# One exponential per key tile, written as 32-bit words and split by halves

## The chip, the cores and the metric

The kernel runs on one core of a Trainium2 chip. The metric is device time in microseconds from start to end of one execution; the number quoted is the median of several executions. The engines are PE (TensorE, matmuls), PEld (its loads of stationary operands), DVE (VectorE), ACT (ScalarE), POOL (GpSimd) and SP (SyncE, which issues the DMAs).

## What is computed

The reference is a clustered attention followed by a soft mixture of experts. For each of 4 x 8 heads, 768 queries and 768 keys of 64 elements are assigned to the nearest of 16 centroids; a query sees the keys of its own cluster alone.

```
mask = q_assign[:, :, :, None] == k_assign[:, :, None, :]
scores = np.where(mask, scale * q @ k.T, -1e9)
attn = np.exp(scores - scores.max(-1))
attn = attn / (attn.sum(-1) + 1e-9)
x = attn @ v                     # -> 3072 rows of 512
logits = x @ phi                 # 32 slots
slot_input = softmax(logits, 0).T @ x
h = relu(slot_input[e] @ w1[e]); slot_out[e] = h @ w2[e]
out = softmax(logits, 1) @ slot_out
```

All inputs and the output are float32.

## The kernel before

The 32 heads are walked in order, in pairs. Scores are made transposed: a key tile has 128 keys on the partitions and 768 queries along the row, six key tiles (j) per head (i). For each head PE does three things. Pass A (`pass_a`, L695) makes untransposed scores, whose row maxima DVE takes (`rowmax`, L703). Pass B (`pass_b`, L737) makes the transposed scores of one key tile in a PSUM buffer `pb` (two of them take turns), with mask and row maximum folded in by extra rows of the operands. Pass C (`pass_c`, L798) multiplies the exponentials by the values and sums over key tiles: the exponentials are the stationary operand, 128 queries at a time, and 64 or 65 columns of values move through them.

Float32 precision is kept by pairs of float16 numbers. Before the change one key tile costs two exponentials on ACT (`expo`, L764): one rounds to float16, which is the high part `EH`, one writes float32, and a subtraction (`elow`, L767) of the two gives the low part `EL` in float16. For most tiles the float32 lies in SBUF (`E32`) and POOL subtracts; for the others, marked D in `LOWS`, `FIRST_LOWS` and `LAST_LOWS`, the float32 is written back to PSUM and DVE subtracts. Values are split the same way by `scalev`, `splitv_hi` and `splitv_lo` into the tile `vx`, and pass C takes three products per query block:

```
for o, (e, r0, w) in enumerate(((eh, D, W), (eh, 0, D), (el, D, W))):
    nc.tensor.matmul(pc[:, c0:c0 + w], e[:, ts], vx[:, j, r0:r0 + w], ...)
```

Column 64 of the values is constant, so that the sum of the exponentials comes out beside the product; `norm` (L812 to L814, DVE) divides.

The order of the work is set by a planner (class `Plan`). Each operation is entered with its engine, an estimated duration, a key, and what it reads and writes; buffer rings of a given depth (`e32`, `eh`, `el` and others) add the waits for reuse. A list scheduler takes, per engine, the ready operation with the least due time, where the table `K` shifts the due time of each key, and `_wt` entries let an operation wait for a more urgent one. The last head's last tile goes in two halves (`expo_half`, `elow_half`, L776 to L783), so that the end of the attention is short.

Six large buffers (`arena`, w7 to w12 in the programs' names) hold the attention's operands; when their last reader is done, expert weights are loaded into them (L1276, SP). The expert part (`TAIL`) follows in an order written out by hand; its operations `hi` (ACT, L1021) and `lo` (DVE, L1024) split weights into float16 pairs, and eight of them are woven into gaps of the attention (`weave`, from planner time `FILL_FROM` on).

Of the kernel before, what the change touches and what calls it, by code (L numbers as in the profile page):

```python
# [10 lines left out]
F16 = mybir.dt.float16  # L11
AF = mybir.ActivationFunctionType
# [6 lines left out]
VS = 256.0  # L19
# [38 lines left out]
class Plan:  # L58
# [127 lines left out]
    FILL_HIGH, FILL_LOW, FILL_BUSY, FILL_FROM = 0.6, 0.62, 1.7, 60.0  # L186
# [38 lines left out]
def clustered_attention_then_soft_moe(  # L225
# [96 lines left out]
    NE32, NEH, NEL = 4, 6, 4  # L322
# [95 lines left out]
    def dma(o, i):  # L418
# [20 lines left out]
        b1=-1581.1, b2=-1348.93, b3=-1474.85, b4=-772.75, b5=-2796.86, x=-3075.5, el=-2389.91,
        c0=-754.47, c1=-1452.52, c2=-1723.07, c3=-1326.05, c4=-1422.75, c5=-1659.96, norm=-0.36,  # L440
        xtrans0=-3047.02, xtrans_out0=-1797.54, xtrans1=-762.69, xtrans_out1=-3163.12, logits=-3303.75,
        disp=-2092.22, comb=-3215.74, warm=-563.02, load_w=-524.15, p0_load_r=-190.35, p0_sims=-1812.55,
        p0_sims_out=-1246.75, p0_assign=-1916.55, p0_assign1=-1303.5, p0_assign2=-846.55,
        p0_assign3=-1913.5, p0_assign4=-176.75, p0_onehot=-1183.1, p0_onehot_out=-1399.44,
        p1_load_r=-2399.42, p1_sims=-1512.26, p1_sims_out=-634.95, p1_assign=-1481.1,
        p1_assign1=-2773.32, p1_assign2=-1055.87, p1_assign3=-2084.84, p1_assign4=-308.2,
        p1_onehot=-2132.69, p1_onehot_out=-2851.21, h0_split_hi=-1530.33, h0_place1=-416.32,
        h0_split_lo=-2905.16, h0_place2=-2748.93, h0_place_mask=41.5, h0_place3=-2642.86,
        h0_load_v=-2985.05, h0_splitv_hi=-927.37, h0_splitv_lo=-2206.46, h0_maxrow=-590.33,
        h0_maxrow_out=-2498.68, h0_x=-1091.42, h0_el=-2014.91, h0_norm=-2111.78, h0_a0=-2392.32,  # L450
# [308 lines left out]
    def ehigh(i, j):  # L759
        return EH[(NT * i + j) // 2 % (NEH // 2)][:, j % 2, :]  # L760
# [824 lines left out]
```

## Time and profile before

| | |
|---|---|
| time, median of 3 executions | 429.03 us (428.45 to 429.6) |
| profiled execution, span from first to last instruction | 427.3 us |
| profiled execution, its own time | not listed apart from the three |
[...]
| start, up to the steady pattern | 0 to about 56 us |
| pairs of heads in the steady pattern | about 56 to 340 us |
| last heads of the attention | about 340 to 373 us |
| expert part and output | about 373 to 427 us |

The three executions differ by 0.27%. The profile is of one execution; its durations are used below, and the span is compared with the median.

### The profile page before, as it was taken

The numbers are of one execution on the slowest core, as the hardware profiler recorded it, in microseconds if no ns is written. First come the engines' busy times: TensorE is split into PE (matmuls) and PEld (weight loads), VectorE is DVE, ScalarE is ACT, GpSimd is POOL, SyncE is SP. The second block draws the span as 40 slices with busy tenths as digits, with TensorE's granted clock in tenths as the row PEclk, the third lists the DMA queues.
The fourth block names the chain that finished last, engine by engine and source line by source line (L and its number), as shares of the span: only waits on it lengthen the run. The fifth ranks groups of instructions, "written<-read, shape, count | busy, mean of one in ns | idle before, by whom it ended". The sixth has DMA issues, their size and how long they took to land.

```text
span 427.3 us, 16090 instructions
## 1 busy us (share of the span) xinstructions
PE 411.3 (96%) x6535; PEld 298.3 (70%) x6535; DVE 381.3 (89%) x749; ACT 371.0 (87%) x597; POOL 328.1 (77%) x267
## 2 busy tenths in 40 slices
PE   8989999999999999999999999999999999899991
PEld 8747677777776777777776777777767777642671
DVE  5889999999999999999999999999999977679972
ACT  5378999999999899999998999999989999849741
POOL 8669999899988798989897889897986688326000
PEclk9999999999999999999999999999999999999998
DMA  6675466566567646667575565665656643899977
GB/s 194 146 226 135 120 156 203 142 198 173 156 182 191 172 104 160 205 162 208 152 216 156 154 167 138 167 173 155 176 158 177 167 148 124 292 356 385 371 307 290
DMA packets 43901, 81.84 MB, mean 192 GB/s; under 512 B 8372, under 2 KB 27956, under 8 KB 43828
## 3 DMA queue, kind: packets, MB, share of 16 engines
q1 hardware_dynamic: 43828, 80.82, 63.6%
q8 instruction: 51, 0.84, 0.8%
q14 instruction: 22, 0.18, 0.1%
HBM read 52.63 MB, written 6.29 MB: 138 GB/s over the span
## 4 chain that ended last, share of the span: by engine, by line
PE 86%; DVE 5%; ACT 5%; issue 1%; DMA 1%; POOL 0%; SPq 0%; DVEq 0%; POOLq 0%
PE pb L737 27%; PE pc L798 22%; PE pa L695 14%; ACT w L764 3%; PE pso L1421 3%; PE pt L554 3%; PE ph L1380 2%; PE pt L823 2%; PE pc L1331 2%; PE pt L902 2%; PE pt L835 1%; DVE w L767 1%; PE po L1499 1%; PE pt L581 1%; ACT pb L764 1%
## 5 line engine op out<-in xcount | busy, mean ns | idle before, releaser
L764 ACT ACTIVATE w<-pb 128x768 f16<-128x768 f32 (+1 forms) x319 | 242.7, 834 | 15.6 <-PE pb L737 14.2
L767 POOL TENSOR_TENSOR w<-w,w 128x768 f16<-128x768 f32 x128 | 209.1, 1646 | 37.0 <-ACT w L764 28.9
L703 DVE TENSOR_REDUCE siT<-pa 128x1 f32<-128x512 f32 (+1 forms) x288 | 187.9, 682 | 5.6 <-PE pa L695 3.9
L737 PE MATMUL pb<-w 128*128 128x512 f16 x764 | 151.6, 325 | 1.2 <-DVE w L767 0.6
L798 PEld LDWEIGHTS <-w 128*128 128x128 f16 x3456 | 126.9, 97 | 11.1 <-DVE w L783 0.4
L798 PE MATMUL pc<-vx,w 128*128 128x65 f16 x3402 | 133.3, 193 | 0.3 <-DVE w L783 0.2
L737 PEld LDWEIGHTS <-w 128*128 128x128 f16 x764 | 69.9, 97 | 59.8 <-issue 6.0
L695 PE MATMUL pa<-w 128*128 128x512 f16 (+1 forms) x384 | 104.1, 326 | 1.1 <-DVE siT L703 0.8
L767 DVE TENSOR_TENSOR w<-pb,w 128x768 f16<-128x768 f32 x63 | 59.8, 949 | 7.7 <-ACT pb L764 4.6
L650 POOL TENSOR_TENSOR w<-w 128x768 f16<-128x768 f32 x32 | 52.6, 1645 | 2.3
L764 ACT ACTIVATE pb<-pb 128x768 f32<-128x768 f32 x63 | 53.2, 844 | 0.0
L695 PEld LDWEIGHTS <-w 128*128 128x128 f16 x384 | 36.4, 98 | 11.7 <-issue 5.0
L647 POOL CAST w<-w 128x768 f16<-128x768 f32 x30 | 24.7, 824 | 9.5 <-DMA w<-w 6.9
L683 POOL TENSOR_TENSOR vx<-w,vx 128x384 f16<-128x384 f32 x32 | 29.1, 909 | 0.4 <-ACT vx L679 0.4
L1024 DVE SCALAR_TENSOR_TENSOR w<-w,w 128x512 f16<-128x512 f32 x31 | 22.5, 769 | 0.0
L1021 ACT ACTIVATE w<-w 128x512 f16<-128x512 f32 x36 | 20.5, 625 | 1.2 <-PE ph L1380 1.2
L814 DVE TENSOR_TENSOR w<-pc,siT 128x384 f32<-128x384 f32 (+1 forms) x32 | 17.6, 551 | 1.1
L675 ACT ACTIVATE w<-w 128x384 f32<-128x384 f32 x32 | 17.6, 551 | 0.8 <-DMA w<-vt 0.8
L679 ACT CAST vx<-w 128x384 f16<-128x384 f32 x32 | 17.7, 554 | 0.2
L554 PEld LDWEIGHTS <-w 128*128 128x128 f16 x540 | 15.7, 96 | 2.6 <-issue 0.5
L828 ACT COPY xT<-pt 128x384 f32<-128x384 f32 x30 | 15.8, 525 | 0.0
L585 ACT ACTIVATE w<-pt,ohsc 128x768 f16<-128x768 bf16 x15 | 13.6, 904 | 2.4 <-PE pt L581 2.4
(209 smaller groups left out, 391.1 us busy)
## 6 DMA issues: line engine op xcount, KB each, us to landing
w<-qkT SPq DMA_DIRECT2D x32, 384.0 KB
w<-w SPq DMA_DIRECT2D x128, 96.0 KB
w<-w1r SPq DMA_DIRECT2D x38, 312.0 KB
w<-w SPq DMA_DIRECT2D x188, 48.0 KB
w<-w2a SPq DMA_DIRECT2D x16, 512.0 KB
w<-w2b SPq DMA_DIRECT2D x16, 512.0 KB
w<-vt SPq DMA_DIRECT2D x32, 192.0 KB
out<-w SPq DMA_DIRECT2D x10, 512.0 KB
```

The source lines that it names most:

```text
L554: nc.tensor.matmul(ps[:, c0:c0 + 2 * NCL], x[(2 * p + hh) % 3][:, t * P:(t + 1) * P], y, start=(hh == 0 and t == 0 and o == 0), stop=(o == ...
L647: (nc.scalar.copy if e == "ACT" else ENG[e].tensor_copy)(RH[i % 3], R[i % 3])
L650: nc.gpsimd.tensor_sub(RL[i % 3], R[i % 3], RH[i % 3])
L683: nc.gpsimd.tensor_sub(vx[:, :, 0:D], V[i % 2], vx[:, :, D:2 * D])
L695: nc.tensor.matmul(pa[:, c0:c0 + w], q1[:, q0:q0 + P], k1[:, k0:k0 + w], start=True, stop=True)
L703: nc.vector.tensor_reduce(hd[i]["mc"][:, 4 * m + c0:4 * m + c1], pa.rearrange("p (n c) -> p n c", n=c1 - c0), axis=AX.X, op=ALU.max, negat ...
L737: nc.tensor.matmul(pbt[j % 2][:, q0:q1], k_[:, kc], q_[:, q0:q1], start=(o == 0), stop=(o == 1))
L764: nc.scalar.activation(dst, pbt[j % 2][:, 0:S], AF.Exp, scale=SCALE)
L767: (nc.vector if lows(i)[j] == "D" else nc.gpsimd).tensor_tensor(EL[(NT * i + j) % NEL], e32(i, j), ehigh(i, j), op=ALU.subtract)
L798: nc.tensor.matmul(pc[:, c0:c0 + w], e[:, ts], vx[:, j, r0:r0 + w], start=(j == 0 and c0 == 0 and o == 0), stop=(j == NT - 1 and o == 2), ...
L1021: nc.scalar.mul(to, segment(n, s), WS)
L1024: nc.vector.scalar_tensor_tensor(low_of(n, s), segment(n, s), WS, HI[n, s], op0=ALU.mult, op1=ALU.subtract)
```

## The change

ACT now evaluates one exponential per key tile, with a bias of 18.125 added to the exponent, and writes 32-bit integers into a word buffer `EW` (eight of them in a ring, in place of four `E32`, six `EH` and four `EL`). The largest exponential is then some 2 to the 26.15. Read as float16, the upper 16 bits of such a word are the number's upper part times 2 to the -24, with no conversion: the word's upper half is below 2048, and float16 patterns up to there are linear in their bits. The lower 16 bits are an unsigned integer; POOL (the DVE path stays in the code but no tile is marked D any more) multiplies them by 2 to the -24 and writes float16 into the same place. Pass C takes its stationary operand from the words, every second float16, so that its columns lie four bytes apart; and since upper and lower halves now carry the same scale, the lower half meets a second value operand `vw`, the values' high part times 2 to the -16, which ACT makes once per head (`splitv_sc`). `VS` and the constant in `norm` follow. The last tile's two halves take one exponential on ACT and one conversion on DVE each. The table `K` is new throughout, and `FILL_FROM` goes from 60 to 90.

```diff
-VS = 256.0
+VS = 1024.0
+EB = 18.125
+EL1 = 2.0 ** -24
+VL1 = 2.0 ** -16
...
-LOWS = ('PDPDPP', 'PDPDPP')
-LAST_LOWS = "PDPDDD"
-FIRST_LOWS = ("PPPDPP", "PPPDPP")
+LOWS = ('PPPPPP', 'PPPPPP')
+LAST_LOWS = "PPPPPP"
+FIRST_LOWS = ("PPPPPP", "PPPPPP")
...
-    FILL_HIGH, FILL_LOW, FILL_BUSY, FILL_FROM = 0.6, 0.62, 1.7, 60.0
+    FILL_HIGH, FILL_LOW, FILL_BUSY, FILL_FROM = 0.6, 0.62, 1.7, 90.0
...
-    NE32, NEH, NEL = 4, 6, 4
+    NEW = 8
...
+    VWs = [area(3, 7 + n, 1)[:, 0:NT * (D + 2)].rearrange("p (t d) -> p t d", d=D + 2) for n in range(2)]
...
-    E32 = [area(n, c, 2, F32) for n, c in ((2, 4), (2, 6), (2, 8), (3, 7))]
-
-    EH = [area(4, 2 * n, 2).rearrange("p (t s) -> p t s", t=2) for n in range(NEH // 2)]
-    EL = [area(4, NEH + n, 1) for n in range(NEL)]
+    EWAT = ((4, 0), (4, 2), (4, 4), (4, 6), (4, 8), (2, 4), (2, 6), (2, 8))
+    EW = [area(n, c, 2, F32) for n, c in EWAT]
...
+        nc.gpsimd.memset(VWs[n][:, :, D:D + 1], VS * VL1)
...
+    def splitv_sc(i):
+        nc.scalar.mul(VWs[i % 2][:, :, 0:D], VXs[i % 2][:, :, D:2 * D], VL1)
...
-    def e32(i, j):
-        if lows(i)[j] == "D":
-            return pbt[j % 2][:, 0:S]
-        return E32[e32n[NT * i + j] % NE32]
+    def words(i, j):
+        return EW[(NT * i + j) % NEW].bitcast(I32)
+
+    def pieces(i, j, dt=F16):
+        return EW[(NT * i + j) % NEW].bitcast(dt).rearrange("p (s k) -> p s k", k=2)
...
-    def ehigh(i, j):
-        return EH[(NT * i + j) // 2 % (NEH // 2)][:, j % 2, :]
-
     def expo(i, j):
-        for dst in (ehigh(i, j), e32(i, j)):
-            nc.scalar.activation(dst, pbt[j % 2][:, 0:S], AF.Exp, scale=SCALE)
+        nc.scalar.activation(words(i, j), pbt[j % 2][:, 0:S], AF.Exp, bias=EB, scale=SCALE)
 
     def elow(i, j):
-        (nc.vector if lows(i)[j] == "D" else nc.gpsimd).tensor_tensor(
-            EL[(NT * i + j) % NEL], e32(i, j), ehigh(i, j), op=ALU.subtract)
+        (nc.vector if lows(i)[j] == "D" else nc.gpsimd).tensor_scalar(
+            pieces(i, j)[:, :, 0], pieces(i, j, U16)[:, :, 0], EL1, 0.0, op0=ALU.mult, op1=ALU.add)
...
     def expo_half(i, j, u):
-        if u == 1:
-            nc.scalar.activation(seg(ehigh(i, j), u), half(u), AF.Exp, scale=SCALE)
-        nc.scalar.activation(half(u), half(u), AF.Exp, scale=SCALE)
-
-    def ehigh_half(i, j, u):
-        nc.vector.tensor_copy(seg(ehigh(i, j), u), half(u))
+        nc.scalar.activation(seg(words(i, j), u), half(u), AF.Exp, bias=EB, scale=SCALE)
 
     def elow_half(i, j, u):
-        nc.vector.tensor_tensor(seg(EL[(NT * i + j) % NEL], u), half(u), seg(ehigh(i, j), u), op=ALU.subtract)
+        nc.vector.tensor_scalar(pieces(i, j)[:, u * HS:(u + 1) * HS, 0], pieces(i, j, U16)[:, u * HS:(u + 1) * HS, 0],
+                                EL1, 0.0, op0=ALU.mult, op1=ALU.add)
...
-        eh, el, vx = EH[n // 2 % (NEH // 2)][:, j % 2, :], EL[n % NEL], VXs[i % 2]
+        e, vx, vw = pieces(i, j), VXs[i % 2], VWs[i % 2]
         for t in range(NT) if u is None else range(u, NT, 2):
             ts = slice(t * P, (t + 1) * P) if u is None else slice(u * HS + t // 2 * P, u * HS + (t // 2 + 1) * P)
             pc, c0 = (hd[i]["pcs"][t % 2], t // 2 * W) if two else (hd[i]["pc"], t * W)
-            for o, (e, r0, w) in enumerate(((eh, D, W), (eh, 0, D), (el, D, W))):
-                nc.tensor.matmul(pc[:, c0:c0 + w], e[:, ts], vx[:, j, r0:r0 + w],
+            for o, (k, v, r0, w) in enumerate(((1, vx, D, W), (1, vx, 0, D), (0, vw, 0, W))):
+                nc.tensor.matmul(pc[:, c0:c0 + w], e[:, ts, k], v[:, j, r0:r0 + w],
...
-        nc.vector.tensor_scalar_add(z, pv[:, :, :, D], VS * 1e-9)
+        nc.vector.tensor_scalar_add(z, pv[:, :, :, D], VS * EL1 * 2.718281828459045 ** EB * 1e-9)
...
+            op("ACT", 0.42, "splitv_sc", h0, lambda i=i: splitv_sc(i), [("vx", i)], [("vw", i)])
...
-                        op("ACT", 0.9 if u else 0.45, "x", t, lambda i=i, j=j, u=u: expo_half(i, j, u), [("pbu", u)],
-                           (ring if u else []) + [("eu", u)])
-                        if u == 0:
-                            op("DVE", 0.5, "el", t, lambda i=i, j=j, u=u: ehigh_half(i, j, u), [("eu", u)], ring[:1] + [("eu", u)])
+                        op("ACT", 0.45, "x", t, lambda i=i, j=j, u=u: expo_half(i, j, u), [("pbu", u)],
+                           ring[:1] + [("eu", u)])
...
+                op("ACT", 0.74, "x", t, lambda i=i, j=j: expo(i, j), [("pb", n)], [("ew", n)])
                 if lows(i)[j] == "D":
-                    op("ACT", 1.395, "x", t, lambda i=i, j=j: expo(i, j), [("pb", n)], [("eh", n), ("pb", n)])
-                    op("DVE", 0.87, "el", t, lambda i=i, j=j: elow(i, j), [("pb", n), ("eh", n)], [("el", n)])
+                    op("DVE", 0.87, "el", t, lambda i=i, j=j: elow(i, j), [("ew", n)], [("el", n)])
                 else:
-                    m = e32n[n] = len(e32n)
-                    op("ACT", 1.395, "x", t, lambda i=i, j=j: expo(i, j), [("pb", n)], [("e32", m), ("eh", n)])
-                    op("POOL", 1.58, "el", t, lambda i=i, j=j: elow(i, j), [("e32", m), ("eh", n)], [("el", n)])
+                    op("POOL", 0.87, "el", t, lambda i=i, j=j: elow(i, j), [("ew", n)], [("el", n)])
                 op("PE", 0.553, f"c{j}", h0, lambda i=i, j=j: pass_c(i, j),
-                   [("eh", n), ("el", n), ("vx", i), ("pc", i)] + ([("flc", 0)] if end else []),
+                   [("ew", n), ("el", n), ("vx", i), ("vw", i), ("pc", i)] + ([("flc", 0)] if end else []),
...
-        c0=-754.47, c1=-1452.52, c2=-1723.07, c3=-1326.05, c4=-1422.75, c5=-1659.96, norm=-0.36,
...
+        h2_b3=-1170.54, h2_b4=-1548.42, h2_b5=-3005.88, h2_c0=-2432.74, h2_c1=-1059.02, h2_c2=-1774.13,
```

The planner's order moves with it. The first place is ACT's row of work where the first head's exponentials begin. `pb0` and `pb1` are the two score buffers, w9, w10 and w11 three of the large buffers, `pt` the one-hot masks of the next pair. Before:

```order
L727 ACTIVATE w9_90<-pb1_116 1x384 x2
L585 ACTIVATE w10_91<-pt_448,ohsc_70 128x768
L764 ACTIVATE w11_92<-pb0_115 128x768
L764 ACTIVATE w9_90<-pb0_115 128x768
L764 ACTIVATE w11_92<-pb1_116 128x768
L764 ACTIVATE w9_90<-pb1_116 128x768
```

After the change, the same place on ACT:

```order
L732 ACTIVATE w9_90<-pb1_118 1x384 x2
L766 ACTIVATE w11_92<-pb1_118 128x768
L587 ACTIVATE w10_91<-pt_459,ohsc_70 128x768
L766 ACTIVATE w11_92<-pb0_117 128x768
L766 ACTIVATE w11_92<-pb1_118 128x768
L766 ACTIVATE w11_92<-pb0_117 128x768
L766 ACTIVATE w9_90<-pb1_118 128x768
```

The first exponential has moved ahead of the copy of the one-hot masks (L585, now L587), and each score buffer is read once, not twice.

The second place is POOL's row in the steady pattern, some ten rows that belong to a little over one head. The L647, L650 and L683 rows are the float16 copy and low part of Q and K and the low part of the values. Before:

```order
L647 CAST w7_88<-w7_88 128x768
L650 TENSOR_TENSOR w8_89<-w7_88 128x768
L767 TENSOR_TENSOR w11_92<-w10_91,w11_92 128x768
L767 TENSOR_TENSOR w11_92<-w9_90,w11_92 128x768 x3
L683 TENSOR_TENSOR vx_1_113<-w8_89,vx_1_113 128x6x64
L767 TENSOR_TENSOR w11_92<-w10_91,w11_92 128x768
```

After the change, with the same three operations at L649, L652 and L685:

```order
L649 CAST w7_88<-w7_88 128x768
L652 TENSOR_TENSOR w8_89<-w7_88 128x768
L685 TENSOR_TENSOR vx_0_111<-w8_89,vx_0_111 128x6x64
L769 TENSOR_SCALAR w11_92<-w11_92 128x768 x3
L769 TENSOR_SCALAR w9_90<-w9_90 128x768
```

Four or so subtractions of two operands per head have become six conversions of one, each in place in its word buffer.

The third place is the end of the attention on ACT, from the last but two key tiles on. Before:

```order
L764 ACTIVATE w11_92<-pb1_116 128x768
L764 ACTIVATE pb1_116<-pb1_116 128x768
L764 ACTIVATE w11_92<-pb0_115 128x768
L764 ACTIVATE pb0_115<-pb0_115 128x768
L777 ACTIVATE pb1_116<-pb1_116 128x384
L776 ACTIVATE w11_92<-pa1_118 128x384
L777 ACTIVATE pa1_118<-pa1_118 128x384
```

After the change:

```order
L766 ACTIVATE w9_90<-pb1_118 128x768
L766 ACTIVATE w11_92<-pb0_117 128x768
L825 COPY xT1_110<-pt_7508 128x384
L777 ACTIVATE w9_90<-pb1_118 128x384
L777 ACTIVATE w9_90<-pa1_120 128x384
L766 ACTIVATE w9_90<-pb0_117 128x768
```

The two halves of the last tile (L777) now stand ahead of the last whole tile, the one before it in the sum, whose lower half is POOL's last conversion.

## Rows read from the trace of the kernel before

**Rows 1.** The page: span, and each engine's busy time.

```profile
span 427.3 us, 16090 instructions
PE 411.3 (96%) x6535; PEld 298.3 (70%) x6535; DVE 381.3 (89%) x749; ACT 371.0 (87%) x597; POOL 328.1 (77%) x267
```

**Rows 2.** Chain that ended last, 56 to 340 us: shares, one piece (start, length).

```profile
by line: PE pb L737 36.4%; PE pc L798 30.3%; PE pa L695 18.5%; PE pt L554 4.0%; PE pt L823 3.0%; PE pt L902 2.3%; PE pt L835 2.1%; PE pt L581 1.5%; PE pt L714 1.0%; PE pt L875 0.6%; PE pt L872 0.3%; issue 0.0%
...
120.15 1.44 PE pb L737 x8
```

**Rows 3.** The same chain, 20 to 56 us.

```profile
by line: PE pb L737 26.4%; PE pc L798 16.8%; PE pa L695 15.6%; ACT w L764 7.8%; DVE siT L703 7.7%; PE pt L554 4.6%; POOL w L650 4.6%; DVE w L767 2.6%; ACT w L585 2.5%; PE pt L581 2.4%; issue 2.2%; DVE pt L565 1.6%; DVE pt L570 1.6%; DVE siT
...
25.66 2.81 ACT w L764 x4
```

**Rows 4.** The same chain, 342.2 to 373.3 us.

```profile
by line: ACT w L764 36.0%; DVE w L767 15.4%; ACT pb L764 10.8%; issue 9.6%; PE pb L737 7.3%; DVE w L1024 5.1%; DVE w L814 4.8%; PE pa L695 2.4%; DVE w L783 2.0%; ACT vx L679 2.0%; DVE siT L813 1.9%; DVE w L780 1.5%; DVE siT L812 1.1%; PE pa
```

**Rows 5.** Chain in order of time, one pair of heads, 231.7 to 253 us.

```profile
231.82 0.89 PE pt L554 x36
...
237.09 0.34 PE pt L581 x6
...
239.49 0.33 PE pt L823 x3
...
247.25 1.11 PE pc L798 x36
248.36 0.65 PE pb L737 x4
...
252.93 0.09 PE pt L554 x4
```

**Rows 6.** Windows: busy us (instructions) of PE, PEld, DVE, ACT, POOL; clock, DMA share, GB/s.

```profile
342.00:373.00 31.00, 29.26 (x503) 22.01 (x499) 22.45 (x39) 30.05 (x47) 21.40 (x15) 1.00 0.56 187
...
370.00:405.00 35.00, 34.22 (x484) 17.83 (x486) 30.57 (x75) 25.23 (x61) 9.89 (x17) 1.00 0.99 371
```

**Rows 7.** Groups by line and form: out<-in, count, busy us, mean ns; idle before.

```profile
L764 ACT ACTIVATE w<-pb 128x768 f16<-128x768 f32 x191 | 159.1, 833 | 15.6 <-PE pb L737 14.2 <-POOL w L767 0.2
L764 ACT ACTIVATE w<-pb 128x768 f32<-128x768 f32 x128 | 106.8, 834 | 0.0
L764 ACT ACTIVATE pb<-pb 128x768 f32<-128x768 f32 x63 | 53.2, 844 | 0.0
...
L679 ACT CAST vx<-w 128x384 f16<-128x384 f32 x32 | 17.7, 554 | 0.2
...
L767 POOL TENSOR_TENSOR w<-w,w 128x768 f16<-128x768 f32 x128 | 209.1, 1646 | 37.0 <-ACT w L764 28.9 <-DVE siT L703 1.9 <-ACT xT L828 1.9
L650 POOL TENSOR_TENSOR w<-w 128x768 f16<-128x768 f32 x32 | 52.6, 1645 | 2.3
L683 POOL TENSOR_TENSOR vx<-w,vx 128x384 f16<-128x384 f32 x32 | 29.1, 909 | 0.4 <-ACT vx L679 0.4
L647 POOL CAST w<-w 128x768 f16<-128x768 f32 x30 | 24.7, 824 | 9.5 <-DMA w<-w 6.9 <-DMA w<-qkT 1.8 <-issue 0.8
...
L767 DVE TENSOR_TENSOR w<-pb,w 128x768 f16<-128x768 f32 x63 | 59.8, 949 | 7.7 <-ACT pb L764 4.6 <-PE pc L798 1.3
```

**Rows 8.** Groups of weight loads by line and form (rows x columns, type).

```profile
L798 PEld LDWEIGHTS <-w 128*128 128x128 f16 x3456 | 126.9, 97 | 11.1 <-DVE w L783 0.4 <-issue 0.3
...
L823 PEld LDWEIGHTS pt<-ident,w 128*128 128x128 f32 x90 | 11.2, 141 | 1.4
...
L1421 PEld LDWEIGHTS <-w 128*32 128x32 bf16 x96 | 1.8, 96 | 0.8 <-issue 0.3
```

**Rows 9.** Chain in order of time, 7 to 9 us: float32 matmuls, 128 weights, 32 columns.

```profile
7.61 1.33 PE pt L591 x12
```

**Rows 10.** Windows of lines L798, then L737 alone, 342 to 373 us.

```profile
342.00:373.00 31.00, 14.61 (x384) 13.56 (x380) 1.00 0.56 187
...
342.00:373.00 31.00, 12.50 (x64) 6.00 (x64) 1.00 0.56 187
```

More of the change, by code (lines that the diff above doesn't have):

```diff
@@ L11 @@
 F16 = mybir.dt.float16
+I32 = mybir.dt.int32
+U16 = mybir.dt.uint16
 AF = mybir.ActivationFunctionType
@@ new lines, in clustered_attention_then_soft_moe @@
+        const6=-1044.52, const9=-2731.44, h0_sims=-2494.06, h1_sims=-2443.21, h0_assign1=-2333.46,
+        h0_assign2=-516.44, h0_assign3=-2529.58, h1_assign1=-2696.57, h1_assign2=-734.39,
+        h1_assign3=-1337.48, h0_onehot=-1457.34, h0_onehot_out=-2765.81, h1_onehot=-1431.93,
+        h1_onehot_out=-1809.37, const=-2763.86, const1=-1541.01, const2=-566.36, load_r=-1694.69,
+        sims=-2592.52, sims_out=-2919.8, assign=-1534, assign1=-2001.48, assign2=-3012.88,
+        assign3=-3219.57, assign4=-152.75, onehot=-2252.72, onehot_out=-4042.04, split_hi=-1262.07,
@@ new lines, in clustered_attention_then_soft_moe @@
+        p0_onehot_out=-1998.94, p1_load_r=-2631.65, p1_sims=-2385.28, p1_sims_out=-634.95,
+        p1_assign=-1481.1, p1_assign1=-3152.73, p1_assign2=-2526.84, p1_assign3=-1909.13,
+        p1_assign4=-308.2, p1_onehot=-3037.17, p1_onehot_out=-1455.75, h0_split_hi=-2021.69,
+        h0_place1=-2663.29, h0_split_lo=-2535.2, h0_place2=-4200.41, h0_place_mask=41.5,
+        h0_place3=-3714.84, h0_load_v=-2185.11, h0_splitv_hi=-3052.6, h0_splitv_lo=-2754.32,
+        h0_maxrow=-2319.67, h0_maxrow_out=-926.74, h0_x=-1010.67, h0_el=-3729.84, h0_norm=-3032.86,
@@ new lines, in clustered_attention_then_soft_moe @@
+        h3_split_lo=-1256.42, h3_place2=-1445.27, h3_place_mask=-1180.48, h3_place3=-876.77,
+        h3_load_v=-2953.38, h3_splitv_hi=-673.01, h3_splitv_lo=-266.72, h3_maxrow=-961.01,
+        h3_maxrow_out=-2034.15, h3_x=-1592.82, h3_el=-1279.46, h3_norm=-1397.97, h3_a0=-2234.38,
+        h3_a1=-1520.89, h3_a2=-1156.03, h3_a3=-2719.37, h3_a4=-3211.15, h3_a5=-3309.57, h3_a6=-2362.73,
+        h3_a7=-1862.43, h3_a8=-2128.17, h3_ra0=-1180.81, h3_ra1=-1010.17, h3_ra2=-678.32,
+        h3_ra3=-2524.91, h3_ra4=-1981.12, h3_ra5=-2033.79, h3_ra6=-2174.95, h3_ra7=-2406.4,
@@ new lines, in clustered_attention_then_soft_moe @@
+        maxrow_wt=1.5, norm1_wt=0.2, norm2_wt=0.4, norm3_wt=0.5, norm5_wt=0.2, o1_a6_wt=0.4,
+        o1_b0_wt=0.2, o1_b5_wt=0.5, o1_c2_wt=0.6, o1_c3_wt=0.1, o1_c4_wt=0.7, o1_load_v_wt=1.5,
+        o1_maxrow_out_wt=0.6, o1_norm_wt=0.7, o1_place3_wt=0.4, o1_ra0_wt=0.2, o1_ra2_wt=0.5,
+        o1_split_hi_wt=0.9, o1_splitv_hi_wt=1.4, onehot_out_wt=0.7, p1_assign2_wt=0.4,
+        p1_assign3_wt=0.4, p1_load_r_wt=0.6, p1_onehot_out_wt=1.4, place1_wt=1.1, place3_wt=0.5,
+        place_mask_wt=0.9, ra3_wt=0.5, ra4_wt=0.6, ra6_wt=0.7, ra7_wt=0.6, split_lo_wt=0.7,
@@ L1304, in rings, with ew @@
         return [(c * HS, 2 * HS, plan.touching((k, b0 - n))) for n, c in enumerate(at) if c is not None]
-    ends = range(plan.last["e32"] - NE32 + 1, plan.last["e32"] + 1)
+    def ew(n):
+        ends = range(plan.last["ew"] - NEW + 1, plan.last["ew"] + 1)
+        return [(EWAT[v % NEW][1] * HS, 2 * HS, plan.touching(("ew", v))) for v in ends if EWAT[v % NEW][0] == n]
     held = (
@@ L1312, in clustered_attention_then_soft_moe @@
         rings("q2", NH - 1, None, 0, 2)
-        + [((4 + 2 * (v % NE32)) * HS, 2 * HS, plan.touching(("e32", v))) for v in ends if v % NE32 < 3],
+        + ew(2),
         rings("q1", NH - 1, 0, 5) + rings("q2", NH - 1, 2) + [(4 * HS, HS, plan.touching(("ohs", NH // 2 - 1)))]
-        + [(7 * HS, 2 * HS, plan.touching(("e32", v))) for v in ends if v % NE32 == 3],
-        last("eh", NEH, 1, *range(NEH)) + last("el", NEL, 1, *range(NEH, NEH + NEL)),
+        + last("vw", 2, 1, 7, 8),
+        ew(4),
         last("xn", 5, 2, 6, 8, 0, 2, 4) + spares(("fin", 0), ("fin", 5), ("pl", NH // 2 - 1)),
```

166 lines of the change are left out of this document (69 added, 97 removed).

## The prediction

> **What bounds the kernel now.** I read the page's busy shares first. PE shows 96%, DVE 89%, ACT 87%, POOL 77% [rows 1]; four engines that close together don't say which sets the time, and PE's share is flattered because the ends of matmuls are modelled and overlap. So the chain that ended last decides, read by stretch. From 56 to 340 us, two thirds of the span, every named piece of the chain is a PE line and "issue" is 0.0% [rows 2]: whatever ACT, DVE and POOL do there is ready before PE wants it. The chain of one pair of heads shows how tight that is: PE goes from the sims of one pair at 231.82 to those of the next at 252.93, 21.1 us, in pieces of 36 pass C matmuls in 1.11 us (30.8 ns each), four score matmuls in 0.65 us and the like, end to end [rows 5]. Faster exponentials can buy almost nothing in this stretch.
>
> They can buy something at its two ends. From 20 to 56 us the chain has ACT's exponentials with 7.8%, DVE's low halves with 2.6% and DVE's row maxima with 7.7%; its longest ACT piece is 2.81 us, four exponentials in a row at 25.66 [rows 3]. From 342.2 to 373.3 us the chain is mostly not PE: ACT's exponentials 36.0% and 10.8%, DVE's low halves 15.4% [rows 4]. ACT is busy there for 30.05 of 31.00 us [rows 6]. After 373 us comes the expert part, which the change leaves alone but for what sits in the buffers it loads into.
>
> **The change, part by part.**
>
> *ACT.* A key tile now costs one exponential in place of two. Rows of before: 191 + 128 exponentials into SBUF at 833 and 834 ns and 63 into PSUM at 844 [rows 7]. 191 of them go, 159 us of busy time. Added are 32 scalings of 128x384 (the new second value operand); the nearest row is the cast of the same shape, 554 ns [rows 7], so 18 us. That the exponential writes 32-bit integers is not in the trace. Float16 and float32 outputs cost the same in the rows just named, so the output type has not mattered; I take 0.83, with 0.84 (the PSUM form) as the other end. A one-column bias is free by the same argument.
>
> *POOL.* 128 two-input subtractions at 1646 ns go; 191 one-input conversions come, of 768 unsigned 16-bit numbers four bytes apart into float16 in the same place. Nearest rows: a one-input cast of the same 768 columns takes 824 ns, a two-input operation 1646 [rows 7]. Bounds 0.82 and 1.65; I take 0.85, since what is new has one input and one output. Per head POOL then has 6 x 0.85, plus 1.65 and 0.91 for low parts of Q/K and V and 0.82 for the cast: 8.5 us of PE's 10.55. *DVE* loses 63 subtractions of 949 ns [rows 7], 60 us, and gains two half-size conversions at the very end. All of these lie beside PE's work in the long stretch and cost or give nothing there.
>
> *PE.* The same 3456 pass C matmuls with the same columns; the number of rows doesn't change. What is new is the stationary operand: 128 float16 columns that lie four bytes apart. No row of before has that. Nearest rows from both sides: the packed float16 load takes 97 ns, as long as a bfloat16 load of only 32 columns (96), while the float32 loads of 128 columns, whose elements do lie four bytes apart, take 141 [rows 8]. [...]
>
> [...]
>
> *The new priorities* move instructions. At the start ACT's first exponential now stands ahead of the one-hot copy, and tiles follow one per instruction. At the end the two half tiles come ahead of the last whole tile, whose lower half POOL makes. In the long stretch the pieces per pair are the same with fewer changes of kind.
>
> **The sum,** against the profiled span of 427.3 us [rows 1], in which PE is already the chain for 284 us.
> - Start: of the 2.81 us of four exponentials half is gone (1.4), DVE's 2.6% of 36 us (0.95) turns into POOL work beside ACT, but the row maxima (2.8 us of chain) stay and are late next. I take 2.0; ends 0 and 3.7 (2.8 of ACT plus 0.95).
> - Long stretch: two score tiles in a row take 1.44 us in one place where twice 0.65 is 1.30 [rows 2, 5]; if each pair hides 0.2 us of such waits (an estimate), 13 pairs give 2.7. The other end is zero, since changes of order can open new waits as well. I take 1.0.
> - End: between 342 and 373 us PE has 384 pass C and 64 score matmuls out of 503 [rows 6, 10]. At the pace of the pair they need 384 x 30.8 ns = 11.8 and 16 x 0.65 = 10.4 us; the other 55 come to some 5.3 at 0.1 each, an estimate from the transposes (0.33 for three [rows 5]). 27.5 of 31.0: 3.5 us idle. POOL's conversion (0.85) between exponential and pass C is what the last tile waits for next. I take 2.5; ends 0 and 3.5.
> - Expert part: from 370 to 405 us the DMA engines are busy 0.99 of the time [rows 6]. The loads wait for the attention's buffers, so they move with its end, but they can't run faster: I give back 0.5; ends 0 and 2.
>
> 2.0 + 1.0 + 2.5 - 0.5 = 5.0, so a span of 422.3. The timed executions have a median of 429.03, 1.7 above the profiled span (that execution's own time is not listed), so 424.0 us. From the ends: nothing won and 2 given back, 431.0; all won, 3.7 + 2.7 + 3.5, 419.1.
>
> **The rivals.**
> - *Pass C's weights load slowly (slower than before).* What such a load does to the pace can be read where float32 weights of 128 columns meet only 32 moving columns: 12 such matmuls take 1.33 us, 111 ns each [rows 9], against 0.89 us for 36 with packed float16 weights and the same 32 columns, 25 ns [rows 5]. Transposes with 128 float32 columns have the same 110 ns pace (0.33 for three [rows 5]), so it is not columns but the weights that set the 111. With two passes per float32 matmul (an estimate: 128 columns at twice the 57 ns which 6 bfloat16 transposes of 128 columns show in 0.34 us [rows 5]) one load is 55 ns. Pass C would go from 30.8 to 55.5 ns: 3456 x 24.7 ns = 85 us, 428 + 85 = 513 us; with 111 ns even 705. The point that decides is small: 5.0 us over 3456 matmuls, 1.45 ns each. For it: the step is that of float32. [...]
> - *POOL becomes the bound (slower).* Its head is 3.38 + 6x us; it passes PE's 10.55 at x = 1.2 us. At the two-input price, 1.65, a head takes 13.3 us: 2.7 x 30 heads = 82 us, 511 us. Against: with one input the rows say 0.82.
> [...]
> - *Nothing comes of it.* PE is the chain anyway; the waits at both ends go over to row maxima on DVE and to POOL's conversions ahead of the last pass C, or DMA holds the expert part: 428 to 430 us.
>
> **How the numbers follow.** A difference under 0.3% (1.3 us) can't be told from none. The forecast, PE's pace unchanged and part of the waits at the ends won, has 0.70, with a range of its own of 419 to 428. No change has 0.10. The slow weight load has 0.14, POOL 0.04, and another 0.02 is for waits that the new order opens, some 432 us. So faster 0.70, same 0.10, slower 0.20. The first two cases hold 8 in 10 together: the range is 418 to 431, by the ends of the sum and a microsecond below, and takes in nothing of the two far rivals.
>
> **What would show it.** Right: pass C's rows still at 30 to 31 ns from start to start and loads at 97 ns; POOL's conversion at 0.8 to 1.0 us; ACT's busy time near 230 us and DVE's near 320, with the pair still at 20.9 to 21.2 us; the chain from 342 us on made of PE; the last pass C some 5 us earlier. Wrong: a pair of 26 us (weight loads) or a chain of POOL rows; a conversion over 1.2 us; a chain in which DVE's row maxima or the DMA take over the ends.

## The result, and the profile after

The changed kernel takes 424.62 us (median of 17 executions, 422.66 to 429.36); the kernel before, run beside it, 428.55 us (17 executions, 427.7 to 429.79). The ratio is 0.990, with a 95% interval of 0.988 to 0.992: faster by about 1% (the ratio leaves out the two slowest executions of the changed kernel, 429.3 and 429.4). The first execution that was profiled took 429.3 us, the long end of that spread, so the profile read here is that of another execution of the same kernel, which took 422.75 us with a span of 421.0 us (run e1 below). That is 1.9 us under the median, so the 6.3 us between the two profiles' spans are more than the 3.9 us between the medians.

The page, engine by engine; it answers to [rows 1]:

```profile
span 421.0 us, 15786 instructions
...
PE 406.2 (96%) x6535; PEld 296.0 (70%) x6535; DVE 327.6 (78%) x685; ACT 263.3 (63%) x437; POOL 314.6 (75%) x332
```

ACT lost 108 us of busy time and DVE 54; PE lost 5 and is still at 96% of a span that is 6.3 us shorter. ACT's and DVE's relief was not the gain in itself: it counted only where work that PE needs had waited for them, which is read stretch by stretch below.

Groups by line and form on PEld, POOL and ACT, with count, busy time and mean duration (answering to [rows 7, 8]):

```profile
L795 PEld LDWEIGHTS <-w 128*128 128x128 f16 x3456 | 124.8, 98 | 11.5 <-issue 0.6 <-POOL w L769 0.2
...
L769 POOL TENSOR_SCALAR w<-w 128x768 f16<-128x768 uint16 x191 | 196.7, 1070 | 45.3 <-ACT w L766 44.8
...
L766 ACT ACTIVATE w<-pb 128x768 int32<-128x768 f32 x191 | 150.7, 810 | 99.1 <-PE pb L742 79.2 <-POOL w L769 17.1 <-POOL w L652 2.0
...
L677 ACT ACTIVATE w<-w 128x384 f32<-128x384 f32 x32 | 16.6, 519 | 11.9 <-DMA w<-vt 11.9
```

The weight load with columns four bytes apart takes 98 ns, the packed one took 97. The exponential that writes int32, with its bias, takes 810 ns; the two of before, without bias, took 833 and 834 [rows 7]. POOL's conversion takes 1070 ns. One wait is new: ACT idles 11.9 us ahead of its scaling of the values (L677) for the value loads (0.8 us before the change), and the exponentials that stand behind that scaling in ACT's order come after it (the rows from 260.29 on, below).

Where the 6.3 us came from is read from four marks. The score matmuls of the clusters (`sims`, L554 and now L556) open each pair; in the chain in order of time, the third and the fifteenth pair of before begin at

```profile
55.83 0.89 PE pt L554 x36
...
319.88 0.89 PE pt L554 x36
```

and after the change at

```profile
52.13 0.89 PE pt L556 x36
...
316.71 0.89 PE pt L556 x36
```

The last weight load of pass C gives the fourth mark; first and last start stand behind the durations. Before:

```profile
L798 PEld LDWEIGHTS <-w x3456: 95/97/103, 29.2 to 372.7; 128*128 128x128 f16 x192
```

After:

```profile
L795 PEld LDWEIGHTS <-w x3456: 96/97/102, 27.4 to 366.8; 128*128 128x128 f16 x192
```

| stretch | before | after (e1) | difference | forecast |
|---|---|---|---|---|
| start to third pair | 55.8 | 52.1 | -3.7 | -2.0 |
| third to fifteenth pair | 264.1 | 264.6 | +0.5 | -1.0 |
| fifteenth pair to last pass C | 52.8 | 50.1 | -2.7 | -2.5 |
| expert part to the end | 54.6 | 54.2 | -0.4 | +0.5 |

Each column is one execution. Two more profiles of the changed kernel show how far the differences hold: in run e10 (423.36 us) they are -2.8, +0.2, -2.7 and -0.5, in the first profile (429.3 us) -2.7, +2.2, +1.2 and -0.5. What the first profile lost lies in the two middle rows.

The end of the attention was mostly ACT in the chain of before [rows 4]. Now the chain from 336.2 to 367.3 us, and two pieces of it in order of time, is PE but for some 2.4% at its very end, where DVE's `norm` follows the last pass C:

```profile
by line: PE pb L742 38.0%; PE pc L795 37.1%; PE pa L700 9.1%; PE pa L795 4.4%; PE pt L820 3.3%; PE pt L832 3.0%; DVE w L811 1.2%; PE pt L1038 1.1%; PE pb L752 1.0%; PE pa L752 1.0%; PE pt L719 0.7%; DVE siT L810 0.6%; DVE siT L809 0.6%; iss
...
355.18 1.30 PE pb L742 x8
...
357.03 0.65 PE pb L742 x4
```

Two score tiles in a row take 1.30 us there, twice the 0.65 of one: no wait between them. ACT is busy for 22.35 us of the last 31 us up to the last pass C, where it was 30.05 [rows 6]; the columns are PE, PEld, DVE, ACT and POOL as in rows 6:

```profile
336.00:367.00 31.00, 31.00 (x563) 24.16 (x560) 17.31 (x37) 22.35 (x37) 23.75 (x23) 1.00 0.50 157
```

In the long stretch score tiles waited before the change and do not now. Before, two tiles in a row take 1.44 us and not 1.30 in eight of the twelve pairs, and single tiles take 0.72 to 0.76 us and not 0.65 in fifteen places. In the first place below the second tile starts at 254.45 in the trace, right behind an exponential that ends at 254.40; the tile of the second place starts at 273.13, right behind a subtraction on DVE that ends at 273.08. So pass B waited there for its score buffer. Before:

```profile
253.82 1.44 PE pb L737 x8
...
273.21 0.73 PE pb L737 x4
```

After, where every such piece in the chain of the twelve pairs but one takes 0.65 or 1.30:

```profile
183.46 1.30 PE pb L742 x8
```

A pair takes 20.98 us (182.13 less 161.15 below), against 21.1 before [rows 5], but not everywhere. Between 248.40 and 292.67 two pairs take 44.3 us and not 42.0, and there the chain of after, read from 56 to 340 us, has two long DMA rows:

```profile
161.15 0.89 PE pt L556 x36
182.13 0.89 PE pt L556 x36
...
248.40 0.89 PE pt L556 x36
...
260.29 6.27 DMA w<-w1r
267.05 6.37 DMA w<-vt
273.87 0.80 ACT w L766
...
292.67 0.89 PE pt L556 x36
```

That is the new wait: before, this stretch was PE alone [rows 2]. It comes back in the other profiles of the changed kernel: the same two pairs take 43.9 us in e10 and 44.0 us in the first profile, with the late value load (L546) in the chain each time, first e10's row, then the first profile's:

```profile
269.08 4.95 DMA w<-vt
...
270.25 5.84 DMA w<-vt
```

So this wait belongs to the new order and not to one execution. The first profile has others besides, among them 5.39 us for a placement (DMA) at 320.84, behind the fifteenth pair.

### The profile page after: what moved, and what is told of

The parts are those of the page before. It is cut to its first block, busy times and chain, and to the rows that moved or that the text cites. A ratio compares the mean times of both kernels' runs of the same rounds, so it can differ in the third digit from the quotient of the medians.

```text
span 427.5 us, 15786 instructions
## 1 busy us (share of the span) xinstructions
PE 407.3 (95%) x6535; PEld 296.1 (69%) x6535; DVE 327.7 (77%) x685; ACT 264.3 (62%) x437; POOL 314.5 (74%) x332
## 4 chain that ended last, share of the span: by engine, by line
PE 81%; DMA 5%; DVE 5%; POOL 3%; ACT 1%; SPq 1%; issue 1%; DVEq 0%; POOLq 0%
PE pb L742 25%; PE pc L795 22%; PE pa L700 13%; PE pso L1418 3%; DMA w<-w 3%; DMA w<-vt 3%; POOL w L769 2%; PE ph L1377 2%; PE pt L556 2%; PE pt L820 2%; PE pt L832 2%; PE pt L899 2%; DVE siT L708 1%; PE po L1496 1%; PE pt L583 1%
## 5 line engine op out<-in xcount | busy, mean ns | idle before, releaser
L769 POOL TENSOR_SCALAR w<-w 128x768 f16<-128x768 uint16 x191 | 196.6, 1071 | 48.3 <-ACT w L766 47.7
L766 ACT ACTIVATE w<-pb 128x768 int32<-128x768 f32 x191 | 150.8, 810 | 98.7 <-PE pb L742 78.2
L742 PE MATMUL pb<-w 128*128 128x512 f16 x764 | 150.3, 326 | 2.4 <-ACT w L766 2.2
L795 PEld LDWEIGHTS <-w 128*128 128x128 f16 x3456 | 125.4, 98 | 12.4 <-issue 0.9
L795 PE MATMUL pc<-vx,w 128*128 128x65 f16 x2268 | 125.7, 193 | 0.0
L795 PE MATMUL pc<-w,w 128*128 128x65 f16 x1134 | 120.4, 194 | 0.7 <-POOL w L769 0.7
L742 PEld LDWEIGHTS <-w 128*128 128x128 f16 x764 | 71.9, 98 | 60.4 <-issue 3.7
L700 PE MATMUL pa<-w 128*128 128x256 f16 (+1 forms) x384 | 101.5, 327 | 0.2
L652 POOL TENSOR_TENSOR w<-w 128x768 f16<-128x768 f32 x32 | 52.7, 1647 | 2.5
L700 PEld LDWEIGHTS <-w 128*128 128x128 f16 x384 | 33.9, 98 | 12.0 <-issue 6.3
L685 POOL TENSOR_TENSOR vx<-w,vx 128x384 f16<-128x384 f32 x32 | 28.7, 896 | 5.4 <-ACT vx L681 5.3
L649 POOL CAST w<-w 128x768 f16<-128x768 f32 x30 | 24.8, 827 | 9.3 <-DMA w<-w 9.1
L677 ACT ACTIVATE w<-w 128x384 f32<-128x384 f32 x32 | 16.6, 519 | 17.6 <-DMA w<-vt 17.5
L723 DVE TENSOR_SCALAR w<-pt 6x128 f16<-6x128 f32 x31 | 8.6, 278 | 11.7 <-PE pt L719 10.1
L688 ACT ACTIVATE w<-vx 128x384 f16<-128x384 f16 x32 | 16.8, 524 | 0.9
L566 DVE TENSOR_REDUCE siT<-pt 128x24 f32<-128x384 f32 x15 | 8.4, 557 | 11.1 <-PE pt L556 11.1
L556 PE MATMUL pt<-w,w 128*128 128x32 f16 x180 | 15.2, 176 | 1.5 <-POOL w L652 1.5
```

Of the source, the lines that this page charges most:

```text
L556: nc.tensor.matmul(ps[:, c0:c0 + 2 * NCL], x[(2 * p + hh) % 3][:, t * P:(t + 1) * P], y, start=(hh == 0 and t == 0 and o == 0), stop=(o == ...
L649: (nc.scalar.copy if e == "ACT" else ENG[e].tensor_copy)(RH[i % 3], R[i % 3])
L652: nc.gpsimd.tensor_sub(RL[i % 3], R[i % 3], RH[i % 3])
L700: nc.tensor.matmul(pa[:, c0:c0 + w], q1[:, q0:q0 + P], k1[:, k0:k0 + w], start=True, stop=True)
L742: nc.tensor.matmul(pbt[j % 2][:, q0:q1], k_[:, kc], q_[:, q0:q1], start=(o == 0), stop=(o == 1))
L766: nc.scalar.activation(words(i, j), pbt[j % 2][:, 0:S], AF.Exp, bias=EB, scale=SCALE)
```

## The experiments

**e1: the changed kernel once more.**

> The changed kernel once more, for a profile of an execution near its median. Theory A (PE is the chain; what is left of waits in the long stretch is the landing of the value loads, which vary): 423 to 425 us; in this profile ACT's wait for the value loads (17.5 us in 12 places in the first profile) is well under 10 us, the chain from 56 to 340 us is PE for over 95%, and the last pass C starts at 369 to 371 us, not at 373.4. Rival B (the waits of the first profile belong to the order itself): the same 17 us of wait and a last pass C at 373 again, whatever the time.

Measured: 422.94 us (421.88 to 423.92), 0.987 of before (0.985 to 0.989). ACT's wait for value loads was 11.9 us in 11 places, not well under 10; the last pass C came at 366.8, earlier than A said; the chain of the long stretch holds DMA for 4.4%, which leaves PE just short of 95%. A's picture of where PE waits held, its marker (the total of ACT's waits) not. B's figures fall (11.9 us and 366.8), but one of the waits does belong to the order, as the late pair above shows.

**e2 and e7: arithmetic and priorities swapped.**

```
e2 = after, with  K = dict(... of before ..., splitv_sc=-2580.02)
e7 = before, with K = dict(... of after ...), FILL_FROM 90.0
```

> The change with the priorities of before (the scaling of the second value operand put between its neighbours' values; weaving from 90 as after). Theory A (the arithmetic gives the time, the priorities only fit the order to it): 425 to 428 us, so over half of the 4 us lost at most. Rival C (the priorities give the time): 429 us or more, no better than before. Rival D (priorities don't matter): within 0.3% of the changed kernel, 423.5 to 426.

> The kernel before with the new table of priorities (and weaving from 90): two exponentials per tile as before. Rival C (the new priorities give the gain): 421 to 427 us. Theory J (each table fits only the durations that it was made with, so that arithmetic and priorities can't be told apart by swapping them): over 440 us, as the change with the old table took 469.

Measured: e2 469.1 us (466.24 to 471.2), e7 543.85 us (542.92 to 544.79). With the other kernel's table each arithmetic is far slower than either kernel: 40 us lost by the one, 115 by the other. A and D fall by e2; C, whose figure of 429 us or more e2 meets, falls by e7; J holds. The chain of e2's long stretch names DVE's row maxima and the DMA, work that the change did not touch:

```profile
by line: PE pb L744 25.1%; PE pc L797 20.1%; PE pa L702 11.2%; DVE siT L710 8.0%; DMA w<-w 5.2%; SPq L424 4.2%; PE pt L558 2.9%; DVE w L813 2.2%; issue 2.0%; PE pt L834 1.8%; PE pt L822 1.7%; POOL w L771 1.6%; PE pt L901 1.6%; SPq L1272 1.3
```

So these two runs can't split the 4 us into a share of the arithmetic and a share of the table. A table fitted anew to the old arithmetic was not run, and what it would give stays open. The traces say something of the end alone. Between the fifteenth pair and the last pass C, ACT (fourth of the engines) was busy for 51.1 of 52.8 us before:

```profile
319.88:372.70 52.82, 51.08 (x860) 38.47 (x856) 43.31 (x78) 51.12 (x79) 35.91 (x24) 1.00 0.59 182
```

That is more than the 50.1 us that the stretch takes now, and in the long stretch ahead ACT was 95% busy too, so that another order of the same work could hardly have made the end as short.

**e3: the exponential twice, in the middle or at the ends.** The order on every engine stays; a second exponential writes the same words again.

```diff
-        nc.scalar.activation(words(i, j), pbt[j % 2][:, 0:S], AF.Exp, ...)
+        [nc.scalar.activation(words(i, j), pbt[j % 2][:, 0:S], AF.Exp, ...)
+         for _ in range(2 if 4 <= i < 28 and j < 4 else 1)]   # ends: i < 4 or i >= 28
```

> The changed kernel with the exponential of four of six key tiles issued twice, in heads 4 to 27 only (the same words written twice, same order on every engine; 96 more exponentials, some 70 us of ACT at 0.7 to 0.8 us). Theory A (ACT's relief is worth nothing in the long stretch, since PE is the chain): at most 1 us slower than the changed kernel, 424 to 426. Rival E (the relief acts throughout): the time goes back towards before, 427 us or more.

> The changed kernel with every whole-tile exponential issued twice in heads 0 to 3 and 28 to 31 only (47 more exponentials). Theory A (the relief is worth something at the two ends alone): 427 to 430 us, with the chain from 342 to 372 us made of ACT's exponentials again. Rival E (relief throughout): 424 to 425.5, since 24 of 32 heads keep it.

Measured: middle 458.71 us (458.31 to 464.73), ends 445.41 us (442.9 to 446.72). A said that the middle costs 1 us at most; it cost 35.8 for 96 exponentials, 0.37 us each. The ends cost 22.5 for 47, 0.48 each, of which A had said 4 to 7. So A is wrong for the middle and far too low for the ends, though the chain from 362 to 391 us there does have ACT's exponentials on top (41.6%), and E is wrong for the ends: in this order an added exponential costs in both. The chain of the middle kernel at one place shows why:

```profile
200.86 0.66 PE pb L742 x4
...
201.61 0.82 ACT w L766
...
202.45 1.52 ACT w L766 x2
...
204.71 0.81 ACT w L766
```

ACT has idle time (73% busy over this kernel's span), but not here: pass B of two tiles stand close together, and the next pass B needs a score buffer back (18.9 us of PE's waits in this kernel are L742 for L766, in 40 places; 2.0 us in e1). The order was built on buffers that come back after one exponential. ACT's relief is used up in the order, also where the chain names PE alone; the changed kernel's mean busy share of 63% says nothing about that. Two limits: weight and value loads stand in this chain too (DMA, 7.4% and 3.3% from 56 to 340 us), so the 35.8 us are not all waits for buffers; and the run shows what an exponential costs when it is put back into the new order, not what the change gained by taking it out of the old one.

**e5: the step of pass C's stationary columns.**

```diff
-    nc.tensor.matmul(pc[...], e[:, ts, k], v[...], ...)
+    # x = the buffer as float16; lines L798, L800, L802, L804, L806
+    j in (0, 5): e[:, ts, k]   j == 1: x[:, 0:128]   j == 2: x[:, 0:512:4]
+    j == 3: x[:, 0:1024:8]     j == 4: x[:, 0:1536:12]
```

> The changed kernel with pass C taking its stationary operand at another column step for each key tile: 2 elements (4 bytes) for tiles 0 and 5 as in the changed kernel, 1 for tile 1, 4 for tile 2, 8 for tile 3, 12 for tile 4 (tiles 1 to 4 multiply other numbers of the same buffers, so the attention's result is not the reference's). Theory A (the step costs nothing): weight loads of 96 to 99 ns and some 30.5 ns from matmul to matmul for each of the steps, time as the changed kernel, 421 to 425. Rival G (the load is slower with a step but hidden at 4 bytes): loads that get longer with the step, 110 ns and more at 8 and 12, and matmuls at 40 ns or more there; with 55 ns for tiles 3 and 4 some 28 us longer.

Measured: 457.04 us, one execution. Weight loads by line, then the chain's pass C pieces of one head (18 matmuls each):

```profile
L798 PEld LDWEIGHTS <-w 128*128 128x128 f16 x1152 | 43.5, 98 | 5.5
L806 PEld LDWEIGHTS <-w 128*128 128x128 f16 x576 | 39.0, 168 | 1.4 <-POOL w L769 0.4
L804 PEld LDWEIGHTS <-w 128*128 128x128 f16 x576 | 38.8, 166 | 0.9
...
L802 PEld LDWEIGHTS <-w 128*128 128x128 f16 x576 | 23.1, 116 | 0.4
L800 PEld LDWEIGHTS <-w 128*128 128x128 f16 x576 | 21.8, 98 | 1.6 <-issue 0.3
```

```profile
101.14 0.54 PE pc L798 x18
104.32 0.55 PE pc L800 x18
106.39 0.59 PE pc L802 x18
107.31 1.08 PE pc L804 x18
108.61 1.08 PE pc L806 x18
```

Steps of 2 and 4 bytes: 98 ns, 30 ns a matmul. 8 bytes: 116 and 33. 16 and 24 bytes: 166 to 168, and 60 ns a matmul. 1152 matmuls at 30 ns more are 34 us, about this kernel's excess over the changed one (34.1 us over e1's median). So the free step of 4 bytes is as forecast, A's "costs nothing" fails in part at 8 bytes and wholly from 16 on, and G is right there. The slow pace of 60 ns is near the 55.5 ns that the prediction priced for its first rival, though it reasoned from float32 loads and these are float16. The chain of this kernel from 56 to 340 us is PE alone again: with pass C slower in this kernel no transfer came late.

**e6: five forms of POOL's conversion.**

```diff
+    j in (0, 5) L772: tensor_scalar(y, x, EL1, 0.0, mult, add)   # x, y: every second 16 bits
+    j == 1 L774: tensor_scalar(yf, xf, EL1, 0.0, mult, add)      # xf, yf: packed
+    j == 2 L776: tensor_scalar(y, x, EL1, None, mult)
+    j == 3 L778: tensor_copy(y, upper halves)                    # strided in and out
+    j == 4 L780: tensor_scalar(yf, x, EL1, 0.0, mult, add)
```

> The changed kernel with the lower half's conversion on POOL in five forms by key tile, to see what of its 1.07 us is due to what (tiles 1, 3 and 4 convert other numbers, and their pass C takes the upper halves twice, so the result is not the reference's): tiles 0 and 5 as in the changed kernel, 4 bytes apart, two constants; tile 1 packed in and out; tile 2 strided with one constant only; tile 3 a cast without constants, strided in and out; tile 4 strided in, packed out. My estimate was 0.85 us for all. Theory H (the stride costs the 0.25 us above the cast's 0.82): tile 1 at 0.82, the others at 1.07, tile 4 between. Theory I (the second arithmetic step costs it): tiles 2 and 3 at 0.82 to 0.95, tile 1 at 1.07.

Measured: 434.54 us, one execution. Groups on POOL by line and form:

```profile
L776 POOL TENSOR_SCALAR w<-w 128x768 f16<-128x768 uint16 x32 | 75.6, 2362 | 2.0 <-ACT w L766 1.9
L772 POOL TENSOR_SCALAR w<-w 128x768 f16<-128x768 uint16 x63 | 66.6, 1064 | 9.6 <-ACT w L766 9.4
...
L778 POOL CAST w<-w 128x768 f16<-128x768 uint16 x32 | 34.2, 1069 | 2.7 <-ACT w L766 2.7
...
L774 POOL TENSOR_SCALAR w<-w 128x768 f16<-128x768 uint16 x32 | 27.2, 850 | 7.9 <-ACT w L766 7.9
L780 POOL TENSOR_SCALAR w<-w 128x768 f16<-128x768 uint16 x32 | 27.2, 849 | 0.0
```

H holds for the stride and has to be narrowed: only the strided write costs (1064 against 849 with the same strided read and a packed write), the read nothing (849 against 850), so tile 4 is not between but as fast as tile 1. I falls: dropping the second constant does not save time but takes 2362 ns, which H did not say either. The estimate of 0.85 us was right for a packed output and gave the step of the write no price.

**e4, e8, e9, e11: the new waits for transfers.** The changed kernel ran beside e8 and e9 once more:

> The changed kernel beside the next two on the same chip. Since its values' loads, placements and weight loads all land just in time, no theory says which of them is late in a given execution: 422 to 426 us.

Measured: 423.61 us (423.36 to 424.14), within what was expected.

```
e4  : SP issues each value load where the planner has its buffer free (in the trace 14 of them start 1.6 to 6.5 us earlier than in e1)
e8  : preload(q) loads the first half of each piece; the other halves in a lump after the attention
e9  : preload(q) for even q alone, two steps' bytes at once
e11 : preload(q) in two halves, the second four SP transfers later
```

> The changed kernel with the loads of the values (heads 4 to 31) issued on SP as soon as the planner has their buffer free, some 0 to 5 us earlier than in the changed kernel; no other engine's order differs. Theory A (the pair that took 23.3 us instead of 21.0, and ACT's 11.9 us of wait for value loads, come from late issue): 420 to 422 us, 1 to 2.5 us under the changed kernel, ACT's wait for the loads under 4 us, no pair above 21.2 us but for those with the slot sums. Rival F (a load that is issued earlier lands no earlier, since the queue and the weight loads ahead of it decide, or it holds up SP's other transfers): 422.5 to 425 and the wait as before.

> The changed kernel with the expert weights that are fetched during the attention halved (six of the seven buffers; as many transfers on SP, each half as long) and the other halves fetched in a lump when the attention ends. Theory K (the late transfers come from the bytes ahead of them in the queues): no DMA row in the chain from 56 to 340 us, the last pass C at 365.5 us or before (366.9 in the changed kernel's second profile), all executions within 1 us of each other; the total some 5 to 10 us longer, since 3 MB at about 400 GB/s move behind the attention. Theory L (SP's issues, 0.6 us each and one after the other, are what is late): last pass C and DMA rows as in the changed kernel.

> The changed kernel with the weight loads of the attention issued two steps at a time (the same bytes, half as many issues on SP, which is busy with issues for 235 of the 284 us of the long stretch). Theory L (SP's issues are what is late): 420 to 422 us, and no DMA row in the chain. Theory K (the bytes ahead are): no better, 423 to 427, since the pieces ahead of a placement are twice as long.

> The changed kernel with each weight load of the attention cut in two, the second piece issued four SP transfers after the first (the same bytes, some 50 issues more on SP). Theory K (what delays the placements and value loads is the piece of weights ahead of them): 421 to 423 us, waits for value loads under 5 us, no or one DMA row in the chain from 56 to 340 us. Theory L (SP's issues): SP, now busy for some 250 of 284 us, is later still: 425 us or more, with SP and DMA rows in the chain.

Measured: e4 426.08 us (422.54 to 427.75; 0.989 to 0.995 of before, where the changed kernel had 0.985 to 0.989 in e1 and 0.987 to 0.990 beside e8: no faster, rather slower), e8 445.2 (443.88 to 445.55), e9 423.5 (422.19 to 426.65), e11 444.91 (443.85 to 446.38).

e4 refutes the theory that late issue of the value loads is all that is late. They no longer stand in its chain, and ACT's wait for them falls from 11.9 to 6.7 us, but other transfers do, the placements of Q and K behind them above all; from the chain of e4:

```profile
173.25 3.10 DMA w<-w
196.33 5.47 DMA w<-w1r
...
269.09 6.19 DMA w<-w
```

e8 takes half the weight bytes out of the attention, and no DMA row is left in the chain of its long stretch:

```profile
54.20 0.89 PE pt L556 x36
...
316.70 0.89 PE pt L556 x36
```

262.5 us, 2.1 less than in e1 and 1.6 less than before the change. K's other figures missed: the last pass C stays at 366.8 because the start came later, the executions lie within 1.7 us and not 1, and the lump costs 22 us, not 5 to 10: its chain behind 361 us is mostly DMA and SP rows (from 340 to 443 us three DMA lines have 43.6% and SP's issues at L1270 16.7%). e9 has half the weight loads, as issues, and is no faster, as K said; that takes only 26 of SP's 387 issues out of the long stretch. e11 has the same bytes and some 50 issues more and is 21 us slower, as L said. In the changed kernel SP issues without a pause ahead of the value load that came late (rows of SP in order of time):

```profile
260.29 0.60 SPq L1270 DMA_DIRECT2D w<-w1r  x1
260.93 5.07 SPq L424 DMA_DIRECT2D w<-w  x6
266.05 0.90 SPq L1270 DMA_DIRECT2D w<-w1r  x2
267.05 0.37 SPq L546 DMA_DIRECT2D w<-vt  x1
```

Both matter, then: what stands ahead on SP, 0.37 to 0.85 us an issue in these rows, and the weight bytes, which move on the same 16 DMA engines (mean busy share from 56 to 340 us 0.63 in e1, 0.56 in e8 with half the weight bytes). Neither is new: from 56 to 340 us SP's issues, each taken by itself, are 386 with 234 us before the change and 387 with 235 after it, for the same bytes, and before no transfer is in the chain. e8 has SP at 240 us and no late transfer either, so a full SP alone doesn't make one late. What is new is the order and what stands ahead of each transfer in it; that was not tested by itself. Which of the two makes a given transfer late, and so the spread of 422.7 to 429.4 us, stays open. No version here is clearly faster than the changed kernel.

## Why the prediction was right, point by point

- **The bound.** PE's chain set the long stretch and sets most of it still (100% before, some 95% in e1); the gain lies at the start and the end. Right. That ACT's work there "cost or give nothing" was too strong: the score tiles' waits of before went, and in the new order an exponential put back costs (e3).
- **Start, -2.0; measured -3.7**, its far end, and -2.8 and -2.7 in the other two profiles. The four exponentials of [rows 3] are two now (1.41 us at 25.14), as put. The row maxima "stay and are late next" only in part: their share of the chain from 20 to 56 us fell from 7.7% to 5.2%, while DVE's low halves (2.6%) went over to POOL's conversions (2.9%). What is late next is SP, whose placements (L424) have 7.3% as issues and 5.9% as DMA: at this end the DMA does come in, which the prediction had named as a sign of being wrong. From the second pair to the third all three profiles gain 5.4 us (22.9 to 17.5), and no run tells ACT's share of that from DVE's and the new order's; the second pair itself starts 1.7 to 2.7 us later than before, and there the three differ. The chain of after from 20 to 56 us, its shares and one piece:

```profile
by line: PE pc L795 16.9%; PE pb L742 15.0%; PE pa L700 11.8%; SPq L424 7.3%; DMA w<-w 5.9%; DVE siT L708 5.2%; PE pt L556 4.1%; ACT w L766 3.9%; DVE pt L567 3.2%; DVE pt L572 3.2%; DVE siT L574 3.2%; DVE w L577 3.2%; POOL w L769 2.9%; DVE 
...
25.14 1.41 ACT w L766 x2
```

- **Long stretch, -1.0; measured +0.5**, wrong in sign and outside its own ends. The step's mechanism, some 0.2 us of hidden waits a pair, is there: the tiles that took 1.44 and 0.72 to 0.76 us are back at 1.30 and 0.65, some 2.5 us over the twelve pairs, and e8, without late transfers, takes 1.6 us less over the stretch. What failed is the end at zero: "new waits" were named as the reason for it, but they can cost more than the step gains. Transfers that were hidden come onto the path (2.1 us in e1 against e8). The prediction had "the DMA" under what would make it wrong at the ends, with no price.
- **End, -2.5; measured -2.7**, and the chain there is PE, as it was to show. The bound of 3.5 was a little high: 55 matmuls at 0.1 us are 5.5 us and at the 0.11 of the transposes 6.1, not 5.3, which leaves 2.7 to 3.3 us idle.
- **Expert part, +0.5; measured -0.4.** Nothing was given back, so this term too had the wrong sign; why the stretch is 0.4 us shorter is not shown.
- **ACT.** 0.83 forecast, 0.81 measured. Busy time was to be near 230 us and is 263: durations of back-to-back exponentials overlap (four in 2.81 us [rows 3], 0.70 each, not 0.83), so less goes with each. Before, the exponentials together kept ACT busy for 283.9 us, now for 150.7: 133 us less, not 159.
- **POOL's conversion, 0.85; measured 1.07**, still under the 1.2 at which POOL would decide.
- **The weight load, first rival.** Refuted at 4 bytes by 98 ns, with 30.3 ns a matmul in pass C (36 in 1.09 us in the chain of e1), where before it was 97 and 30.8 [rows 5, 8]. That the pace would hold was the author's estimate, and no row of before shows it for such a step. At 16 bytes a load of 166 ns does set the pace, 60 ns a matmul (e5).

That the total, 424.6 against 424.0, is so close is in part luck: against the sum, e1 has 1.7 us more won at the start, 1.5 lost in the long stretch, 0.2 more won at the end and 0.9 in the expert part, which leaves 1.3, and e1 is 1.9 us under the median. So the errors cancel, and the executions of the changed kernel spread over more than the whole gain.

## What to carry to other kernels

Here a stationary operand of 128 float16 columns was read out of wider words at no cost with a step of 4 bytes (98 ns a load, 30 ns a matmul) and at little with 8 (116 and 33); check the pace of the matmuls, since at 16 and 24 bytes it went from 30 to 60 ns each. When an engine off the critical path is relieved, ask what the next order will spend that slack on: here a few transfers, which had been hidden, came onto the path in the new order, one of them in every profile of the changed kernel (the late value load, with rows of 4.95 to 6.37 us). Read more than one execution before a wait is put down to chance or to the order. And a planner's table belongs to the durations that it was fitted to, so swapping one of the two tells nothing of the other's share.

## What was not expected of the hardware

- Stationary loads of 128 float16 columns (e5): 98 ns at steps of 2 and 4 bytes, 116 at 8, 166 and 168 at 16 and 24.
- POOL, 768 16-bit elements (e6): 849 ns with a strided read and a packed write, 1064 with a strided write; multiplication by one constant without a second step, 2362.
- ACT, idle for over a third of the changed kernel's time, still cost 0.37 us of the total for each exponential of 0.81 us that e3 added in the middle.
